# Moving a second level of Strassen from layer 1's fifth product to layer 2's first and fifth products

## The chip, the cores and the metric

The kernel runs on one core of a Trainium2 chip. The metric is the device time of one execution in microseconds (us). The numbers of the profile come from one profiled execution of the same program.

## The reference

Sparse attention over 4 x 8 heads of 768 tokens gives x, 3072 tokens by D = 512. Eight experts (F = 1024) then work on all tokens, and their outputs are added with weights P that come out of eight rounds of row and column scaling:

```python
    logits = x @ w_gate
    P = np.exp(logits - logits.max())
    for _ in range(8):
        P /= P.sum(1, keepdims=True) + 1e-09
        P /= P.sum(0, keepdims=True) + 1e-09
        P *= N / E
    for e in range(E):
        h = np.maximum(x @ w1[e], 0.0)        # layer 1: [3072,512] x [512,1024]
        ye = h @ w2[e]                        # layer 2: [3072,1024] x [1024,512]
        out += P[:, e:e + 1] * ye
```

## The kernel before

**Stages.** Attention and expert 0 take the first part of the span, and the scaling of P follows beside the first products of expert 1. From there on experts 1 to 7 run, in products of fp16 matmuls summed in fp32. This second part is what the change touches.

**Strassen, first level.** Both layers of experts 1 to 7 use the Winograd form of Strassen's algorithm: the operands are cut into 2 x 2 quarters (A11 to A22 the stationary ones, B11 to B22 the moving ones), sums S1 to S4 and T1 to T4 of quarters are formed by VectorE, and seven products p1 to p7 (layer 1) or q1 to q7 (layer 2) take the place of eight. In layer 1 a unit is an expert e, a block j of 512 tokens in each half of the tokens (NJ = 3 blocks), and half u of the hidden columns; a unit, called a *duo*, has two sides k, and each product of a side is two matmuls of 512 columns (`product1`, line 991). There are 42 duos, six for each expert. In layer 2 a pair (e, j, c) is the token tile c of block j and its partner in the other half; each of its seven products is four matmuls of 256 columns (`product2`, line 997). There are four pairs in a block, so two for each duo.

**Strassen, second level.** In `duo`, `second` computes the first product (names ending in m) or the fifth (ending in n) of both sides together by seven pieces instead of eight: each piece is one matmul of 256 columns (line 1050). It starts with piece 1 in one bank, ScalarE copies the half (`fd`, line 1059) into a second bank and `fh` (line 1070) sets another half aside; VectorE adds halves in the joins j1 and j2 (`plus`, line 938). m is used from block (1, 2) on, in 38 duos, and n from block (2, 1) on, in 34. Its sums of weights (`wa_sum`) and of tokens (`xa_sum`) for n (g = 1) live in unused rows of out_acc.

**Banks.** PSUM has eight banks here: ab (three, layer 1's products), g (two, layer 1's second accumulators), x (two) and y (one) for layer 2. After products, ScalarE copies (c5, c2, c1, seeds, v6, r11, r21) and VectorE adds with a clip at zero (`relu_plus`, line 941, c12 and c22) or adds halves (v5). Results hf of layer 1 lie in the tile hs (seven quarters A11, A12, S3, A22, S1, S2, S4), of which there are four.

**Outputs.** For experts 2 to 7 ScalarE scales each quarter by P (`part`, line 1265) into rows c and HT + c of out_acc, and GpSimd's queue adds them to the output in DRAM by DMA (`da` line 1286, `db` line 1289). So most of out_acc is free scratch in these experts. The last block fetches its rows back (`fetch`, line 1242), adds there with VectorE, and stores.

**The order of the work.** `Plan.order` is a planner that runs when the program is built: each step is `put` with an engine, an estimated cost from the table `us`, the steps it depends on, the banks it opens and uses, and a priority. It emits the steps in the order in which its model starts them; every engine then takes its own in that order. Priorities come from the table `PR` (one number for each kind of step). `feed(n)` puts duo n, the weight loads and sums for the next expert and the pairs of duo n - 2, three duos ahead of the one being emitted.

Of the kernel before, what the change touches and what calls it, by code (L numbers as in the profile page):

```python
# [10 lines left out]
FP32 = mybir.dt.float32  # L11
# [129 lines left out]
def kernel(  # L141
# [10 lines left out]
    nc = tc.nc  # L152
# [767 lines left out]
    if True:  # L920
# [107 lines left out]

        def wa_sum(g, e, u, n):
            if n == 0:  # L1030
                wa[g, e, u] = (spare16(HT + 4 + (2 * e + u) % 3, 384).rearrange("p (s f) -> p s f", s=3) if g else
                               late.tile([128, 3, 128], FP16, tag="wa", name="wa", bufs=3))
# [137 lines left out]
        def pair(e, j, c, spare=False, tail=False, c1_at=None):  # L1170
            def h(q):
                return lambda f: hs[e, j, f // 2][:, q, f % 2, :]
            ta, tb = 4 * j + c, HT + 4 * j + c
            B = {}
# [54 lines left out]
            def add_to(t, k, src):  # L1229
                acc = out_acc[:, t, k * DH:(k + 1) * DH]  # L1230
                nc.vector.scalar_tensor_tensor(out=acc, in0=at(src), scalar=P_sb[:, t, e:e + 1], in1=acc,
                                               op0=ALU.mult, op1=ALU.add)
# [4 lines left out]
            def store(t, k=slice(0, DM), eng=nc.sync):  # L1237
                eng.dma_start(out=rows(t)[:, k], in_=out_acc[:, t, k])

            def fetch():  # L1240
                for t in (ta, tb):
                    nc.sync.dma_start(out=out_acc[:, t, :], in_=rows(t))

            def add_less(src):
                acc = out_acc[:, tb, 0:DH]
                nc.vector.scalar_tensor_tensor(out=acc, in0=at(src), scalar=nP_sb[:, tb, e:e + 1], in1=acc,
                                               op0=ALU.mult, op1=ALU.add)
# [46 lines left out]
            def fin():  # L1294
                nc.gpsimd.tensor_tensor(out=out_acc[:, tb, 0:DH], in0=out_acc[:, tb, 0:DH], in1=out_acc[:, tb, DH:DM],
                                        op=ALU.add)
                store(tb)

            def ahead():
                nc.gpsimd.tensor_tensor(out=out_acc[:, tb, 0:DH], in0=out_acc[:, tb, 0:DH], in1=out_acc[:, tb, DH:DM],  # L1300
                                        op=ALU.add)

            def z3():
                nc.scalar.activation(out=out_acc[:, HT + 7, c // 2 * DH:(c // 2 + 1) * DH], in_=at(3), func=AF.Copy, scale=P_sb[:, ta, e:e + 1])
# [5 lines left out]
            def z0():  # L1310
                nc.vector.scalar_tensor_tensor(
                    out=out_acc[:, tb, 0:DH], in0=at(2), scalar=P_sb[:, tb, e:e + 1],
                    in1=out_acc[:, tb, 0:DH], op0=ALU.mult, op1=ALU.add)

            def z4():
                nc.gpsimd.tensor_tensor(out=out_acc[:, ta, DH:DM], in0=out_acc[:, ta, DH:DM], in1=out_acc[:, HT + 7, c // 2 * DH:(c // 2 + 1) * DH], op=ALU.add)
# [5 lines left out]
            def x1():  # L1322
# [3 lines left out]
            return {f.__name__: f for f in (scale_a, scale_b, q1, c1, q5, v5, q6, v6, q2, q7, q3, q4, y0, y1, y2, y3, fin, ahead, fetch, e0, e1, e2, e3, e4,  # L1326
                                            da, db, dc,
                                            z3, z2, z0, z4, x0, x1)}

        us = dict(m=0.1092, p=0.4316, q=0.4368, seed=0.55, c5=0.5, c2=0.49, r=0.49, c12=0.607, c22=0.607, s=0.6,  # L1330
                  c1=0.34, v6=0.28, v5=0.35, y=0.395, half=0.275, join=0.335, w1=0.205, w2=0.6, wa=0.14, x=0.6,
# [138 lines left out]
        for u in course:  # L1470
# [7 lines left out]
        plan.more({"x": 2, "y": 1, "c1": 1, "m5": 1, "n5": 1})  # L1478
        plan.ring["ab"].append(None)

        PR = {
# [13 lines left out]
        pairs = {}  # L1495

# [3 lines left out]
        def w_sums(e, i, prio, old=()):  # L1500
            for n in range(4):
                WT[e, i, n] = put("DVE", us["w1"], lambda n=n: w1_sum(e, i, n),
                                  [WT.get((e, i, n - 1)), U["w1", e, i], *old], prio + 0.01 * n)

# [20 lines left out]
        def pair_users(e, j, names=("q1", "q2", "q3", "q4", "q5", "q6", "q7")):  # L1525
            return [pairs[e, j, c][q] for c in range(4) for q in names] if (e, j, 0) in pairs else []

        def plan_pair(e, j, c, prio):
# [5 lines left out]
            f, d = pair(e, j, c, spare, last_block, c1_at), {}  # L1534
# [5 lines left out]
            def op(name, eng, cost, deps, opens=(), uses=(), p=None):  # L1540
# [7 lines left out]
            op("q1", "PE", m, of("r110", "r111") + [U["w2", e]] + ([src[1]["c121"], src[1]["r211"]] if spare else []),  # L1548
               [bx])
            op("c1", "ACT", us["c1"], ["q1"] + ([src[1]["c121"], src[1]["c221"]] if spare else []), c1s, [bx])  # L1550
            op("q5", "PE", m, ["q1", W2[e, 0]] + of("s1"), (), [bx])
            op("v5", "DVE", us["v5"], ["q5", "c1"], [by], [bx] + c1s)
# [11 lines left out]
            if spare:  # L1564
                op("ahead", "POOL", 0.75, [pairs["in", c]], p=0)
                op("z3", "ACT", us["part"], ["q3"], (), [by], p=1)
# [5 lines left out]
            elif e == 1 or last_block:  # L1572
# [7 lines left out]
                else:  # L1580
                    pairs["ys", c] = pairs["st", c] = landed([d["y2"], d["y3"]], 4.0)
            else:
                free = [pairs["ys", c]] if e > 2 or j else [pairs[1, 0, c]["landed"]]
                op("e0", "ACT", us["part"], ["q2"] + free, (), [bx], p=PR["yd"])
                op("e2", "ACT", us["part"], ["q7"] + free, (), [by], p=PR["yd"] + 2)
                if e < E - 1:
                    op("e1", "ACT", us["part"], ["q4"] + free, (), [bx], p=PR["yd"] + .1)
                else:
                    op("e4", "DVE", us["y"], ["q4", "e2"] + free, (), [bx], p=PR["yd"] + 2)
                op("e3", "ACT", us["part"], ["q3"] + free, (), [by], p=PR["yd"] + 2.1)  # L1590
                op("da", "POOL", us["da"], ["e0", "e3"], p=PR["yd"] + 3)
                op("db", "POOL", us["da"], ["e1" if e < E - 1 else "e4", "e2"]
                   + ([pairs["dc", j, c]] if e == E - 1 else []), p=PR["yd"] + 3)
                pairs["ys", c] = landed([d["da"], d["db"]], 4.0)
                if e == E - 2 and j < NJ - 1:
                    op("dc", "POOL", us["da"], [pairs["ys", c]], p=PR["yd"] + 160)
                    pairs["dc", j, c] = landed([d["dc"]], 4.0)
                if e == E - 2 and j == NJ - 1:
                    op("fetch", "SP", 0.2, [pairs["ys", c]], p=PR["yd"])
                    pairs["in", c] = landed([d["fetch"]], 4.0)  # L1600
# [4 lines left out]
            if e == 1:  # L1605
                d["landed"] = pairs["ys", c]
# [5 lines left out]
        def feed(n):  # L1612
            base = 10000.0 + 100.0 * n
            if n < len(duos):
# [7 lines left out]
                for g, h, since in ((0, "m", (1, 2)), (1, "n", (2, 1))):  # L1622
# [4 lines left out]
                def prio(name):  # L1627
                    if name in ("s1", "s3", "s2", "s4"):
                        return base + PR["S"] + 0.1 * ("s1", "s3", "s2", "s4").index(name)
                    return base + PR[{"p10": "m1", "p11": "m4"}.get(name, name)]  # L1630
# [10 lines left out]
                if n == 7:  # L1641
                    p5s = ("p50", "p51")
                    held = [pairs[1, 1, c]["landed"] for c in range(4)]
                    for v in range(2):
                        wa_sums(1, 2, v, base + 30 + 10 * v, held + users(2, 0, v, p5s))
                    for m, i in enumerate((1, 2, 0)):
                        xa_sums(1, i, base + 50 + 70 * m, held + users(*((2, 0) if i == 0 else (1, i)), 0, p5s)
                                + users(*((2, 0) if i == 0 else (1, i)), 1, p5s))
                if e + 1 < E:
# [11 lines left out]
                    if k == 5:  # L1661
                        w_sums(e + 1, 1, w - 100, users(e, 2, 0))
                        for g in (0, 1) if e > 1 else (0,):
                            wa_sums(g, e + 1, 0, w - 90, users(e - 1, 2, 1))
# [3 lines left out]
                        for g in (0, 1) if e > 1 else (0,):  # L1668
                            wa_sums(g, e + 1, 1, w + 20, users(e, 2, 0))
            m = n - 2  # L1670
            if m < len(duos):
# [45 lines left out]
```

## Time and profile before

| | |
|---|---|
| median of 3 runs (lowest to highest) | 664.56 us (664.53 to 665.34) |
| the profiled execution | 664.45 us, its span 662.7 us |
| TensorE, weight loads, VectorE, ScalarE, GpSimd busy | 652.9, 456.8, 506.0, 533.2, 260.0 us |
| matmuls of layer 2 (line 997) | 2352 of 128x256, 273 ns each |
| matmuls of layer 1 (line 991) | 888 of 128x512, 379 or 380 ns each |
| pieces of the second level (line 1050) | 504 of 128x256, 273 ns each |
| joins m (pab<-pab,m) and n (pab<-pab,out_acc) | 76 and 68, 427 and 431 ns each |
| half copies (line 1059; line 1070 to m and to out_acc) | 72; 38 and 34, 380 ns each |
| layer 1's sums (hf<-hf 128x1024) | 126 and 42, 687 and 682 ns each |
| granted TensorE clock | 0.999 |

Busy times are sums in which overlapping instructions of one engine count once. Successive matmuls overlap: each one's row holds its passage through the array, so the distance between starts, not the length, is what one costs in a stream. In the chain that ended last, TensorE has 89% of the span.

### The profile page before, as it was taken

To read this page: it belongs to the slowest core of one execution; us is meant where nothing else is said; L and a number is where in the kernel's file an instruction comes from. 1 tells how busy PE (TensorE), PEld (TensorE's weight loads), DVE (VectorE), ACT (ScalarE), POOL (GpSimd) and SP (SyncE) were. 2 spreads that over 40 slices of the span, in tenths; PEclk is the share of its full clock that TensorE was granted. 3 is DMA by queue.
4 is the path that set the end of the run, shared out by engine and by line. 5 is a ranking of instruction groups with operands and counts; after the bars stand their busy time and mean duration, and the time that the engine had idled before them with its cause. 6 is when DMAs were issued, how large, how long until landed. Compare 5 with 4: busy or idle time off the path is not lost.

```text
span 662.7 us, 14448 instructions
## 1 busy us (share of the span) xinstructions
PE 652.9 (99%) x5293; PEld 456.8 (69%) x5293; DVE 506.0 (76%) x1304; ACT 533.2 (80%) x1189; POOL 260.0 (39%) x322
## 2 busy tenths in 40 slices
PE   8999999999999999999999999999999999999996
PEld 4766656555677677777777777777777777777775
DVE  7889998579889987685767767866768576776674
ACT  6776766556995678998989989899899898998872
POOL 8699504223011022444343342534343445533322
PEclk9999999999999999999999999999999999999999
DMA  9999958600627268986979697988898598988676
GB/s 162 185 153 148 143 82 82 87 2 1 111 98 142 96 121 122 126 106 83 170 100 132 87 156 97 128 101 117 135 126 111 74 185 114 153 137 175 90 90 165
DMA packets 147078, 77.70 MB, mean 117 GB/s; under 512 B 112704, under 2 KB 124736, under 8 KB 147008
## 3 DMA queue, kind: packets, MB, share of 16 engines
q0 software_dynamic: 124864, 62.64, 81.2%
q1 hardware_dynamic: 21184, 13.42, 8.1%
q8 instruction: 41, 0.67, 0.4%
q10 hardware_dynamic: 960, 0.74, 0.4%
q14 instruction: 29, 0.24, 0.1%
HBM read 55.59 MB, written 45.09 MB: 152 GB/s over the span
## 4 chain that ended last, share of the span: by engine, by line
PE 89%; DVE 8%; DMA 1%; issue 0%; ACT 0%; DVEq 0%
PE px L997 21%; PE pg L991 16%; PE py L997 16%; PE pab L991 12%; PE pab L1050 8%; PE yps L236 5%; PE hps L226 5%; DVE xs L552 1%; DMA kT<-kst 1%; PE sg L388 1%; PE idle L597 1%; PE tkq L354 1%; DVE em L440 1%; DVE km L382 1%; PE pab L997 1%
## 5 line engine op out<-in xcount | busy, mean ns | idle before, releaser
L997 PEld LDWEIGHTS <-hf 128*128 128x128 f16 x2352 | 229.9, 98 | 79.5 <-issue 0.8
L1289 POOL DMA_DIRECT2D out_dram<-out_acc x68 | 60.0, 883 | 209.3 <-ACT out_acc L1265 193.1
L997 PE MATMUL px<-w,hf 128*128 128x256 f16 x656 | 98.3, 273 | 0.0
L997 PE MATMUL px<-ws,hf 128*128 128x256 f16 x656 | 97.8, 273 | 0.0
L997 PE MATMUL py<-w,hf 128*128 128x256 f16 x656 | 91.2, 273 | 0.0
L935 DVE TENSOR_TENSOR hf<-hf 128x1024 f16<-128x1024 f16 x126 | 83.4, 687 | 0.5
L1265 ACT ACTIVATE out_acc<-py,P_sb 128x256 f32<-128x256 f32 x136 | 61.2, 476 | 24.2 <-PE py L997 21.6
L941 DVE CUSTOM_DVE_ANT_0 hf<-pab,c 128x512 f16<-128x512 f32 x84 | 57.8, 689 | 25.8 <-ACT c L1123 12.4
L1286 POOL DMA_DIRECT2D out_dram<-out_acc x68 | 69.0, 1014 | 20.4 <-ACT out_acc L1265 19.4
L991 PEld LDWEIGHTS <-w 128*128 128x128 f16 x520 | 50.9, 98 | 20.4
L941 DVE CUSTOM_DVE_ANT_0 hf<-pg,c 128x512 f16<-128x512 f32 x84 | 57.7, 686 | 9.4 <-ACT c L1116 5.9
L938 DVE TENSOR_TENSOR pab<-pab,out_acc 128x256 f32<-128x256 f32 x68 | 29.3, 431 | 43.9 <-PE pab L1050 43.9
L938 DVE TENSOR_TENSOR py<-px,c 128x256 f32<-128x256 f32 x82 | 35.0, 427 | 35.9 <-PE px L997 34.9
L202 POOL DMA_DIRECT2D w<-in_moe_w_dram x56 | 44.2, 862 | 42.4 <-PE pg L991 40.9
L991 PE MATMUL pab<-xT,w 128*128 128x512 f16 x184 | 54.6, 380 | 0.0
L217 ACT ACTIVATE hf<-pg 128x512 f16<-128x512 f32 x84 | 50.6, 607 | 4.5 <-PE pg L991 1.8
L1123 ACT COPY c<-pg 128x512 f32<-128x512 f32 x84 | 50.1, 596 | 4.5 <-PE pg L991 2.6
L1108 ACT COPY pg<-pab 128x512 f32<-128x512 f32 x84 | 50.4, 601 | 2.7 <-PE pab L1050 2.7
L217 ACT ACTIVATE hf<-pab 128x512 f16<-128x512 f32 x84 | 50.4, 601 | 2.4 <-PE pab L991 1.8
L1116 ACT COPY c<-pab 128x512 f32<-128x512 f32 x84 | 49.0, 583 | 3.3 <-PE pab L991 2.4
L991 PE MATMUL pab<-xT,ws 128*128 128x512 f16 x168 | 50.0, 379 | 0.0
L991 PE MATMUL pg<-xT,w 128*128 128x512 f16 x168 | 50.0, 379 | 0.0
(191 smaller groups left out, 1388.8 us busy)
## 6 DMA issues: line engine op xcount, KB each, us to landing
out_dram<-out_acc POOLq DMA_DIRECT2D x136, 256.0 KB, 5.3
w<-in_moe_w_dram POOLq DMA_DIRECT2D x8, 1024.0 KB, 9.5
w<-in_moe_w_dram POOLq DMA_DIRECT2D x56, 128.0 KB, 5.7
out_dram<-out_acc SPq DMA_DIRECT2D x28, 256.0 KB, 2.3
vx<-in_v_dram POOLq DMA_DIRECT2D x16, 192.0 KB, 5.7
qst<-in_q_dram POOLq DMA_DIRECT2D x31, 96.0 KB, 5.3
kst<-in_k_dram POOLq DMA_DIRECT2D x24, 96.0 KB, 5.2
out_acc<-out_dram SPq DMA_DIRECT2D x8, 256.0 KB, 4.3
```

What stands on the lines that cost most here:

```text
L217: nc.scalar.activation(out=out, in_=in_, func=AF.Relu, bias=0.0, scale=1.0)
L935: nc.vector.tensor_tensor(out=out, in0=in0, in1=in1, op=ALU.subtract)
L938: nc.vector.tensor_tensor(out=out, in0=in0, in1=in1, op=ALU.add)
L941: nc.vector._custom_dve(TENSOR_ADD_SAT, out=out, in0=in0, in1=in1, s0=FLT_MAX, s1=0.0)
L991: nc.tensor.matmul(bank[:], lhsT=w[:, dk, :], rhs=x[:, dk, :], start=start and dk == 0, stop=dk == KH - 1, skip_group_check=True)
L997: nc.tensor.matmul(bank, lhsT=a(f)[:, 128 * c:128 * (c + 1)], rhs=w[:, f, :], start=start and f == 0, stop=f == FH - 1, skip_group_check=True)
L1050: nc.tensor.matmul(B[bank][:, lo:lo + 256], lhsT=weight1a(g, w, e, u), rhs=moving1a(g, v, j), start=start, stop=True, skip_group_check=True)
L1108: nc.scalar.copy(out=B["g" + K][:], in_=B["a" + K][:])
L1123: nc.scalar.copy(out=B["c2" + K][:], in_=B["g" + K][:])
L1265: nc.scalar.activation(out=out_acc[:, (c, HT + c)[t == tb], k * DH:(k + 1) * DH], in_=at(src), func=AF.Copy, scale=scale[:, t, e:e + 1])
L1286: nc.gpsimd.dma_start(out=rows(ta), in_=out_acc[:, c, :], accum_op=ALU.add)
L1289: nc.gpsimd.dma_start(out=rows(tb), in_=out_acc[:, HT + c, :], accum_op=ALU.add)
```

## The change

Layer 2's first and fifth products of two token tiles c and c + 2 are computed together by a second level (`twin`): the quarters are the two tiles (rows), the two halves of the hidden columns, and the two halves of 128 output columns. One bank holds q1 in its first half and q5 in its second, and each of the seven pieces n1 to n7 is four matmuls of 128 columns (two products, two parts of the sum). Two copies (nd, nh) and two joins (j1, j2) lie between them, as in layer 1. After them the pairs go on as before with c1, v5, q6 and so on. Twins are used in blocks (2, 1) to (7, 1); blocks of expert 1, (2, 0) and the last block keep four matmuls for each product.

VectorE forms the sums: `h_sub`, four for each block, over 128x1024 elements, and `w2_sub`, eight for each expert, over 128x256. S1, S2, S4 lie in three rows of out_acc; S3 takes the place of quarter A21, whose block's later products do not read it. The sums of w2 lie in other rows of out_acc.

Layer 1's fifth product goes back to two matmuls of 512 columns a side; its sums of weights and tokens for g = 1 are gone. PSUM has ab with two banks instead of three, y with two instead of one. The last block's tiles live in other rows of out_acc (`home`), and its `fetch` is put with tiles 0 and 2 of block (7, 1) instead of with the pairs of block (6, 2). `z3` waits for the matmuls of block (7, 1). The table PR has a number for each kind of step and an added one for each of the six duos of an expert (`rank`).

The core of the diff:

```diff
+        LAST_A, LAST_B = (11, 21, 0, 2), (20, 22, 12, 23)
+        def h_sub(e, j, n):
+            own = hs[e, j, 0][:, A11:S1 + 1:S1 - A11, :, :], hs[e, j, 1][:, A11:S1 + 1:S1 - A11, :, :]
+            m = {"A11": own[0][:, :, :, 0:256], "A21": own[0][:, :, :, 256:512], "S3": own[0][:, :, :, 256:512],
+                 "A12": own[1][:, :, :, 0:256], "A22": own[1][:, :, :, 256:512]}
...
+            f(m[o], m[a], m[b])
+        def twin(e, j, c, b0, b1):
...
+            def piece(b, k, w, v, start=False):
+                for g in range(2):
+                    for i in range(2):
+                        nc.tensor.matmul(half(b, k)[:, g, :], lhsT=still2(e, j, g, w, c)[:, i, :],
+                                         rhs=moving2a(e, g, v)[:, i, :], start=start and g == 0 and i == 0,
+                                         stop=i == 1, skip_group_check=True)
-        plan.more({"x": 2, "y": 1, "c1": 1, "m5": 1, "n5": 1})
-        plan.ring["ab"].append(None)
+        plan.more({"x": 2, "y": 2, "c1": 1, "m5": 1, "n5": 1, "k9": 1})
+        TWIN = (2, 1), (E - 1, NJ - 2)
+        def rank(name, k):
+            return PR[name] + PR.get(f"{name}.{k}", 0.0)
+        def plan_twin(e, j, c, prio):
...
+            op("n1", "PE", us["n"], [src[0][x] for x in ("r110", "r111", "s1")] + [W2[e, 0], pairs.get("nd")], [b0])
+            op("nd", "ACT", us["half"], ["n1"], [b1], [b0])
+            op("n5", "PE", us["n"], ["n1", s[0], *t[0]], (), [b0])
+            op("nh", "ACT", us["half"], ["n5"], [kh], [b0])
+            op("n2", "PE", us["n"], ["nd"] + [src[1][x] for x in ("r110", "r111", "s1")], (), [b0])
+            op("n6", "PE", us["n"], ["nd", s[1], *t[1]], (), [b1])
+            op("j1", "DVE", us["join"], ["n6", "nh"], (), [b0, b1, kh])
+            op("n3", "PE", us["n"], ["j1", s[3]], (), [b0])
+            op("n7", "PE", us["n"], ["j1", s[2], *t[2]], (), [b1])
+            op("j2", "DVE", us["join"], ["n7"], (), [b1, kh])
+            op("n4", "PE", us["n"], ["j2", *t[3]], (), [b1])
+            for k in range(2):
+                plan_pair(e, j, c + 2 * k, prio + rank(f"q{k}", 2 * j + c),
+                          (built[k], (b0, b1)[k], ([d["n2"], d["n3"]], [d["n4"]])[k]))
...
-                for g, h, since in ((0, "m", (1, 2)), (1, "n", (2, 1))):
+                for g, h, since in ((0, "m", (1, 2)),):
...
+                if u and TWIN[0] <= (e, j) <= TWIN[1]:
+                    h_sub_sums(e, j, base + rank("NS", j))
+                if e >= 2 and (n == 8 or e > 2 and (j, u) == (0, 0)):
+                    w2_sub_sums(e, base + PR["NW"], [pairs[1, NJ - 1, 3]["landed"]] if n == 8 else [])
-            if m < len(duos):
+            if m < len(duos) and TWIN[0] <= duos[m][:2] <= TWIN[1]:
+                plan_twin(*duos[m], base)
+            elif m < len(duos):
```

More of the change, by code (lines that the diff above doesn't have):

```diff
@@ L1173, in pair @@
             ta, tb = 4 * j + c, HT + 4 * j + c
+            home = {ta: LAST_A[c], tb: LAST_B[c]} if tail else {ta: ta, tb: tb}
             B = {}
@@ new lines, in still2, with w2_subs @@
+        def still2(e, j, g, what, c):
+            lo = 128 * (c % 2)
+            if what in ("S1", "S2", "S4"):
+                return h_subs(e, j)[:, ("S1", "S2", "S4").index(what), g, :, lo:lo + 128]
+            lo += 256 if what in ("A21", "S3", "A22") else 0
+            return hs[e, j, int(what in ("A12", "A22"))][:, (A11, S1)[g], :, lo:lo + 128]
+        def w2_subs(e, g):
+            if e % 2 == 0:
+                a = spare16((11, HT + 11)[g], 1024)
+            elif g:
+                a = spare16(HT + 7, 1024)
+            else:
+                a = out_acc[:, HT + 4:HT + 7, :].rearrange("p t f -> p (t f)").bitcast(FP16)[:, 1152:2176]
+            return a.rearrange("p (s k f) -> p s k f", s=4, k=2)
@@ new lines, in moving2a, with w2_sub @@
+        def moving2a(e, g, what):
+            if what[0] == "T":
+                return w2_subs(e, g)[:, int(what[1]) - 1]
+            k = 2 if what in ("B21", "B22") else 0
+            o = 128 if what in ("B12", "B22") else 0
+            return ws2[e][:, 0, k:k + 2, o:o + 128] if g else w2s[e][:, k:k + 2, o:o + 128]
+        def w2_sub(e, g, n):
+            m = {w: moving2a(e, g, w) for w in "B11 B12 B21 B22 T1 T2 T3 T4".split()}
+            sub(*[m[w] for w in (("T1", "B12", "B11"), ("T2", "B22", "T1"), ("T3", "B22", "B12"),
+                                 ("T4", "B21", "T2"))[n]])
@@ new lines, in twin, with half, open_bank, n1 @@
+        def twin(e, j, c, b0, b1):
+            B = {}
+            def half(b, k):
+                return b["x"][:].rearrange("p (g k f) -> p g k f", g=2, k=2)[:, :, k, :]
+            def open_bank(b):
+                b["x"] = xps.tile([128, 512], FP32, tag=f"x{plan.now.pop(0)}", name="px", bufs=1)
+            def piece(b, k, w, v, start=False):
[4 more added lines that the diff above has]
+                                         stop=i == 1, skip_group_check=True)
+            def n1():
+                open_bank(b0)
+                piece(b0, 0, "A11", "B11", True)
+            def nd():
+                open_bank(b1)
+                nc.scalar.copy(out=half(b1, 0), in_=half(b0, 0))
+            def n5():
+                piece(b0, 1, "S1", "T1")
+            def nh():
+                plan.now.pop(0)
+                B["held"] = out_acc[:, 7, 256:512].rearrange("p (g f) -> p g f", g=2)
+                nc.scalar.copy(out=B["held"], in_=half(b0, 1))
+            def n2():
+                piece(b0, 0, "A12", "B21")
+            def n6():
+                piece(b1, 0, "S2", "T2")
+            def j1():
+                plus(half(b0, 1), half(b1, 0), B["held"])
+            def n3():
+                piece(b0, 1, "S4", "B22")
+            def n7():
+                piece(b1, 0, "S3", "T3")
+            def j2():
+                plus(half(b1, 1), half(b1, 0), B["held"])
+            def n4():
+                piece(b1, 0, "A22", "T4")
+            return {f.__name__: f for f in (n1, nd, n5, nh, n2, n6, j1, n3, n7, j2, n4)}
@@ L1503, in w_sums, with h_sub_sums, w2_sub_sums @@
                                   [WT.get((e, i, n - 1)), U["w1", e, i], *old], prio + 0.01 * n)
+        HS2, W2A = {}, {}
+        def h_sub_sums(e, j, prio):
+            src = [made[e, j, 0], made[e, j, 1]]
+            first = [pairs[1, NJ - 1, c]["landed"] for c in range(3)] if e == 2 else []
+            HS2[e, j] = s = []
+            for n, more in enumerate((first + [src[1][x] for x in ("s1", "r110", "r111")] + [src[0][x] for x in ("s1", "r110", "r111")], [],
+                                      [src[0]["s2"], src[0]["s3"]], [])):
+                s.append(put("DVE", us["ns"], lambda n=n: h_sub(e, j, n), s[-1:] + more, prio + 0.01 * n))
+        def w2_sub_sums(e, prio, old=()):
+            for g in range(2):
+                for n in range(4):
+                    W2A[e, g, n] = put("DVE", us["nw"], lambda g=g, n=n: w2_sub(e, g, n),
+                                       [W2A.get((e, g, n - 1)), W2[e, 0], *old], prio + 0.01 * n + 0.1 * g)
         def wa_sums(g, e, u, prio, old=()):
@@ L1533, in plan_pair @@
                 c1_at = lambda: fast.tile([128, 512], FP32, tag=("c2", "c5")[c // 2], name="c1t", bufs=1)[:, 0:DH]
-            f, d = pair(e, j, c, spare, last_block, c1_at), {}
+            f, d = second[0] if second else pair(e, j, c, spare, last_block, c1_at), {}
             src = [made[e, j, 0], made[e, j, 1]]
@@ L1591, in plan_pair @@
-                op("da", "POOL", us["da"], ["e0", "e3"], p=PR["yd"] + 3)
+                    op("e4", "DVE", us["y"], ["q4", "e2"] + free, (), [bx], p=rank("yd", 4 * j + c) + 2)
+                op("e3", "ACT", us["part"], ["q3"] + free, (), [by], p=rank("yd", 4 * j + c) + 2.1)
+                op("da", "POOL", us["da"], ["e0", "e3"], p=rank("yd", 4 * j + c) + 3)
                 op("db", "POOL", us["da"], ["e1" if e < E - 1 else "e4", "e2"]
-                   + ([pairs["dc", j, c]] if e == E - 1 else []), p=PR["yd"] + 3)
```

134 lines of the change are left out of this document (81 added, 53 removed), and 76 rows, old and new, of the table PR.

## The prediction

> **What bounds the kernel now.** I read the engine shares first, then busy time over the stretch in which the change acts, then TensorE's waits, and last the order of matmuls inside that stretch.
>
> ```profile
> PE 652.9 (99%) x5293; PEld 456.8 (69%) x5293; DVE 506.0 (76%) x1304; ACT 533.2 (80%) x1189; POOL 260.0 (39%) x322
> ```
>
> ```profile
> 250.00:640.00 390.00, 390.00 (x2933) 286.41 (x2931) 279.15 (x642) 349.90 (x841) 153.88 (x182) 1.00 0.88 122
> ```
>
> ```profile
> PE pab L1050 <- DVE pab L938: 0.2, 1, 0.2
> ```
>
> The first line is the page's, the second the busy times from 250 to 640 us (PE, PEld, DVE, ACT, POOL), the third the only wait of TensorE after its first 120 us. In that stretch TensorE has no gap, at full clock; ScalarE is busy 89.7% (349.90/390), VectorE 71.6%. A busy row of matmuls overlaps itself (each lasts 273 ns but they start 109 ns apart), so I test it by starts:
>
> ```profile
> 404.81 0.60 PE L997 MATMUL px<-ws,hf 128*128 128x256 f16 x4
> 405.25 1.04 PE L997 MATMUL py<-w,hf 128*128 128x256 f16 x8
> 406.12 0.59 PE L991 MATMUL pab<-xT,w 128*128 128x512 f16 x2
> ```
>
> Columns are start and length; 406.12 - 404.81 is 1.31 us for twelve 256-column matmuls: 0.109 each. Pairs of 512 columns (L991) take 0.433 us there, 0.2165 each. A duo (two token-tile pairs of layer 2 and one unit of layer 1) has 56 + 14 matmuls of 256 columns and 20 of 512: 70 x 0.109 + 20 x 0.2165 = 11.96 us. The chain of waits shows the same py products at 309.70, 321.66 and 333.64: a period of 11.96 us. So the stretch has no slack: what TensorE has to issue is the time, and what it saves ends the kernel earlier, as long as nothing makes it wait.
>
> **The price of a 128-column matmul.** The whole change rests on it, since layer 2's pieces go from 256 to 128 columns, each with its own weight load. Layer 2 before shows none, but attention does:
>
> ```profile
> 60.94 0.50 PE L354 MATMUL tkq<-ident,qst 128*128 128x128 bf16 x6
> 61.28 0.51 PE L398 MATMUL vs<-vx,m_blk 128*128 128x128 bf16 x6
> 61.62 1.03 PE L236 MATMUL yps<-w,h 128*128 128x512 f16 x4
> ...
> 65.17 0.51 PE L354 MATMUL tkq<-ident,kst 128*128 128x128 bf16 x6
> 65.51 0.50 PE L354 MATMUL tkq<-ident,qst 128*128 128x128 bf16 x6
> 65.85 0.74 PE L573 MATMUL lp<-wg_bf,xT 128*128 128x8 f16 x24
> 66.45 0.32 PE L226 MATMUL hps<-xT,w 128*128 128x384 f16 x1
> ```
>
> Six go by in 0.34 us (60.94, 61.28, 61.62; again 65.17, 65.51, 65.85): 0.0567 each, with one load per matmul. A line through 0.109 at 256 and 0.2165 at 512 gives 0.0553 at 128. I take 0.056 and keep 0.0553 and 0.0567 as ends. Loads alone go faster: 24 matmuls of 8 columns, each with its load, pass in 66.45 - 65.85 = 0.60 us, 25 ns each.
>
> The Trainium skill (TensorE: Matmul & The Clock Gate, Back-to-back issue gap) says that a real stream of weight loads and matmuls holds about 81 ns each at 128 columns, more than the 56 ns of isolated ones; by that figure the change would be an estimated 20 us slower (28 x 0.081 against 1.744, 32 times, and 3.5). The rows above, loads included, disagree with it.
>
> **The change, part by part.**
>
> *Layer 2, q1 and q5 in a twin.* Two token tiles had 2 x 2 x 4 = 16 matmuls of 256 columns: 16 x 0.109 = 1.744 us. A twin has 7 products x 2 x 2 = 28 of 128 columns: 28 x 0.056 = 1.568. It saves 0.176, and there are 32 twins (blocks (2,1) to (7,1) are 16, two twins each): -5.6 us (-6.3 at 0.0553, -5.0 at 0.0567).
>
> *Layer 1's fifth whole.* The n product of a unit had 7 x 0.109 = 0.763 us; whole it is 4 x 0.2165 = 0.866. That costs 0.103 in each of the 34 duos that had it (the 68 joins pab<-pab,out_acc are two each): +3.5 us.
>
> TensorE's sum: -2.1 us (-2.8 to -1.5). Break-even is a piece price of (1.744 - 3.5/32)/28 = 0.0584 us, so the direct rows leave only 3% of room.
>
> *ScalarE.* Out go 34 x 2 half copies (380 ns, L1059 and L1070), in come 32 x 2 (nd, nh) of the same size; c1 stays one per tile. Nothing changes beyond 68 against 64 copies. It stays at 90%, hidden beside TensorE as now.
>
> *VectorE.* Joins: 68 out, 64 in, 0.43 us each. Out per expert: 8 sums wa of g=1, at 0.219: 1.75 us. In per expert of three blocks: 12 sums h_sub of 128x1024 (row hf<-hf, 687 ns): 8.24 us, and 8 sums w2_sub of 128x256 (row ws<-w, 285 ns): 2.28. Net 8.8 us more per six duos (71.8 us): 71.6% becomes 84%. Beside TensorE this costs nothing if it spreads; its cover is VectorE's idle time, 28% now. Uncovered it costs what a sum lasts, 0.69 us at a time. VectorE takes its instructions in order: behind four sums (2.75 us) stand c12, c22, v5 and the joins j1, j2, for which TensorE waits. The window 322 to 334 us has 10.02 us of VectorE work in 12 already; a block's sums fit only in its neighbours with 7.5. I take zero to 0.34 us per block, and zero as likeliest.
>
> *PSUM.* ab goes from 3 banks to 2, y from 1 to 2. A unit's first product needs both ab banks while its split runs, then seed, p2, r11; I bound the hold by the rows: some 3 us for the split's round trips (four matmul stages of about 0.3, copies 0.38, joins 0.43 twice), then 0.6 + 0.6 + 0.6, then b: 0.6 + 0.6 + 0.7 with matmuls between, in all about 8 us of a 11.9 us period. The x pair: split, c1 (0.40), v5 (0.43), two products, two scalings (0.48): about 6 of 11.9. Neither is full, and with the second bank y never holds. Value 0; bounds -0.4 us (one join's wait less at the start) to +2 us (one ScalarE queue late in each of a few duos).
>
> *Order.* Every step after 180 us moves. PE's order before leaves 0.2 us of waits there, so an order cannot gain; it can only lose.
>
> *The end.* The last block's tiles move to other rows of out_acc, and its fetches (eight, 4.3 us to landing, on SP from 587.45 us before) wait: the last two for the landing of tiles 0 and 2 of block (7,1). Before, POOL's adds of that block go out at 636, 641 and 647 us; with 5.3 to landing, four issues of 0.34 and 4.3, data is there at about 647, and the last block's tiles 2 and 3 first use it at 648 to 650. SP has nothing else queued until 650.40. Margin 1 to 3 us; cost 0, at worst +2.
>
> Sum: the profiled execution took 664.45 us (span 662.7 and 1.75 around it), 0.11 below the median of 664.56. 664.45 - 2.1 = 662.35, near 662.4 on the median's scale. About 0.2% (1.3 us) is what a measurement of this kernel can tell from no change.
>
> **The rivals.**
>
> 1. *Gaps of the new order eat the gain* (same). With ScalarE at 90% and VectorE at 84%, an order written ahead by estimates drifts. For: peaks of 10 us in 12. Against: 0.2 us of gaps now. One gap of 0.06 us in each of 32 duos gives 1.9 us back: 664.3.
>
> 2. *VectorE's sums hold TensorE* (slower). Place: the four h_sub sums of each of 16 blocks, ahead of joins and evictions. Price: half a sum, 0.34 us, per block, 5.5 us in all: 664.45 - 2.1 + 5.5 = 667.9. It eats the gain from 0.13 us a block on and is slower by 0.2% from 0.21. For: 84% and the strict queue. Against: TensorE has two duos of work in hand.
>
> 3. *The loads set the pace* (slower). A load row lasts 98 ns; if it showed whole, 28 x 0.098 - 1.744 = 1.0 us per twin, 32 + 3.5 = 35 us: 700; half shown, near 682. Against: the rows of 25 and 57 ns with a load each. For: those runs are six long, and attention's. The Trainium skill's 81 ns (the page and section above) would be this rival.
>
> 4. *The end waits for its fetches* (same): 2 us, 664.4.
>
> **How the numbers follow.** Forecast 0.52 (661.3 to 663.2, likeliest 662.4); rival 1 0.16; rival 2 0.22; rival 3 0.06; rival 4 0.04. Faster 0.52, same 0.20, slower 0.28. The range reaches from 661.3 (0.0553 a piece, and 0.4 at the start) to 668.0 (rival 2 at its price); outside are rival 3 and the worse part of rival 2.
>
> **What would show it.** The 128x128 rows of layer 2 should number 896 and start 0.056 us apart; a duo should take 40 x 0.109 + 28 x 0.056 + 7 x 0.109 + 24 x 0.2165 = 11.89 us; VectorE should stand at 84% with ScalarE at 90%; TensorE's waits should stay under 1 us after 250 us. Wrong: a start distance over 0.058, waits of PE px on DVE h_sub or join rows, or a last block whose first adds wait for a DMA.

## The result, and the profile after

The changed kernel takes 667.43 us (median, 665.13 to 671.63), beside 664.77 us for the kernel before on the same chip: a ratio of 1.0048, 95% interval 1.0026 to 1.0071. Run again beside other kernels, it had 1.0024 (1.0010 to 1.0039). So it is slower by 0.2 to 0.5% where I forecast 0.3% faster. The profiled execution took 669.53 us, its span 667.6, its clock 0.995.

The page's shares and the busy times from 250 to 640 us (PE, PEld, DVE, ACT, POOL) answer to the two lines shown of before:

```profile
PE 652.6 (98%) x5575; PEld 447.4 (67%) x5575; DVE 543.6 (81%) x1352; ACT 531.4 (80%) x1185; POOL 260.4 (39%) x322
```

```profile
250.00:640.00 390.00, 389.51 (x3219) 277.09 (x3217) 320.63 (x708) 349.93 (x842) 154.67 (x182) 1.00 0.87 119
```

In the stretch that the change is about nothing went wrong: TensorE is busy 389.51 of 390 us, ScalarE exactly as before (349.93), VectorE at 320.63/390 = 82%, where I forecast 84%. The loss is not there. TensorE's waits say where it is (total, times, longest, in us):

```profile
PE px L997 <- DVE out_acc L1275: 3.8, 1, 3.8
PE vs L398 <- DMA vx<-in_v_dram: 1.4, 1, 1.4
...
PE px L1397 <- DVE px L938: 0.4, 1, 0.4
```

One wait of 3.8 us, once. (The 1.4 us lie in attention, ahead of all that the change touches: they come and go between executions of the same program.) The trace in order of time (start, length, engine) shows the end of the scaling of P, the pieces, and the wait (lines between are left out at "..."):

```profile
162.28 0.28 PE L1537 MATMUL sink<-csum_sb,col_en 128*128 128x8 f32 x2
...
394.83 0.28 PE L1397 MATMUL px<-w,hf 128*128 128x128 f16 x2
394.94 0.27 PE L1397 MATMUL px<-ws,hf 128*128 128x128 f16 x2
395.05 0.39 PE L1397 MATMUL px<-out_acc 128*128 128x128 f16 x4
395.28 0.27 PE L1054 MATMUL pab<-xa,w 128*128 128x256 f16 x1
...
643.70 1.77 SPq L1247 DMA_DIRECT2D out_acc<-out_dram  x4
...
651.45 0.60 PE L997 MATMUL py<-w,hf 128*128 128x256 f16 x4
...
651.96 0.72 POOL L1306 TENSOR_TENSOR out_acc<-out_acc 128x256 f32<-128x256 f32 x1 [7.06 <-DMA out_acc<-out_dram]
652.71 0.48 DVE L1236 SCALAR_TENSOR_TENSOR out_acc<-pg,P_sb,out_acc 128x256 f32<-128x256 f32 x1 [6.24 <-POOL out_acc L1306]
...
655.33 0.47 DVE L1275 SCALAR_TENSOR_TENSOR out_acc<-px,nP,out_acc 128x256 f32<-128x256 f32 x1
655.86 0.60 PE L997 MATMUL px<-w,hf 128*128 128x256 f16 x4 [3.81 <-DVE out_acc L1275]
...
660.22 1.04 PE L997 MATMUL py<-w,hf 128*128 128x256 f16 x8
```

Eight pieces pass in 395.28 - 394.83 = 0.45 us, 0.056 each, with a load for every one: the price that the change rests on is as forecast. Then read upwards from 655.86. TensorE stands for VectorE's L1275; VectorE, which takes its queue in order, has six additions to the last block ahead of L1275 (it empties the bank px), and stood 6.24 us itself for GpSimd's L1306; that stood 7.06 us for the fetch that SP (the sync engine) issued from 643.70 on. One DMA holds three engines in turn.

To compare kernels I use two marks that every one has: the last `sink` matmul (160.00 before, 162.28 after), up to which the program is the same, and the start of TensorE's last group (655.41 before, 660.22 after). In the trace of before they are

```profile
160.00 0.28 PE L1427 MATMUL sink<-csum_sb,col_en 128*128 128x8 f32 x2
...
655.41 1.04 PE L997 MATMUL pg<-w,hf 128*128 128x256 f16 x8
```

Between them lie 495.41 us before and 497.94 after, 2.53 more. This *stretch* leaves out the 2.28 us of the profiled execution that chance put ahead of the first mark. Each stretch is that of one profiled execution.

| kernel | median us | ratio to before, 95% interval | stretch us | last group to end of span us |
|---|---|---|---|---|
| before | 664.77 to 665.25 | | 495.41 | 7.3 |
| after | 667.43 | 1.0048 (1.0026 to 1.0071) | 497.94 | 7.4 |
| again (after, unchanged) | 666.89 | 1.0024 (1.0010 to 1.0039) | 498.12 | 7.4 |
| early_fetch | 664.73 | 0.9994 (0.9985 to 1.0003) | 494.27 | 8.3 |
| short_sums | 665.78 | 1.0007 (0.9994 to 1.0020) | 496.84 | 7.3 |
| fifth_whole (from before) | 677.50 | 1.0181 (1.0165 to 1.0198) | | |
| late_fetch (from before) | 671.49 | 1.0094 (1.0076 to 1.0111) | 499.59 | 10.2 |
| early_short | 663.85 | 0.9981 (0.9973 to 0.9990) | 493.88 | 8.4 |
| spare_last | 664.70 | 0.9992 (0.9983 to 1.0000) | 494.16 | 8.3 |
| double_sums | 703.57 | 1.0573 (1.0558 to 1.0588) | | |
| early_load | 663.75 | 0.9978 (0.9968 to 0.9987) | 493.35 | 7.7 |
| pool_s4 | 688.70 | 1.0349 (1.0333 to 1.0366) | | |
| pool_s4_load | 687.54 | 1.0330 (1.0313 to 1.0348) | | |

Each ratio is to runs of the kernel before on the same chip: again, early_fetch, short_sums and fifth_whole shared one, so did late_fetch, early_short, spare_last and double_sums, and the last three.

### The profile page after: what moved, and what is told of

Same layout as the page of the kernel before. It is cut to its first block, busy times and chain, and to the rows that moved or that the text cites. A ratio compares the mean times of both kernels' runs of the same rounds, so it can differ in the third digit from the quotient of the medians.

```text
span 667.6 us, 15025 instructions
## 1 busy us (share of the span) xinstructions
PE 652.6 (98%) x5575; PEld 447.4 (67%) x5575; DVE 543.6 (81%) x1352; ACT 531.4 (80%) x1185; POOL 260.4 (39%) x322
## 4 chain that ended last, share of the span: by engine, by line
PE 84%; DVE 6%; DMA 3%; issue 3%; POOL 1%; ACT 1%; POOLq 0%; DVEq 0%
PE pab L991 16%; PE pg L991 16%; PE py L997 15%; PE px L997 12%; PE px L1397 7%; PE yps L236 5%; PE hps L226 5%; PE pab L1054 4%; DVE xs L552 1%; DMA kT<-kst 1%; DMA vx<-in_v_dram 1%; DMA w<-in_moe_w_dram 1%; PE sg L388 1%; PE tkq L354 1%; DVE em L440 1%
## 5 line engine op out<-in xcount | busy, mean ns | idle before, releaser
L997 PEld LDWEIGHTS <-hf 128*128 128x128 f16 x1840 | 178.7, 98 | 52.8 <-issue 4.3
L935 DVE TENSOR_TENSOR hf<-hf 128x1024 f16<-128x1024 f16 x142 | 94.2, 688 | 2.2
L997 PE MATMUL py<-w,hf 128*128 128x256 f16 x656 | 92.5, 273 | 0.0
L991 PEld LDWEIGHTS <-ws 128*128 128x128 f16 x504 | 47.3, 98 | 33.5 <-issue 0.3
L1270 ACT ACTIVATE out_acc<-py,P_sb 128x256 f32<-128x256 f32 x136 | 63.5, 486 | 7.0 <-PE py L997 5.2
L202 POOL DMA_DIRECT2D w<-in_moe_w_dram x56 | 46.8, 935 | 51.8 <-PE pg L991 49.8
L991 PEld LDWEIGHTS <-w 128*128 128x128 f16 x520 | 49.2, 98 | 21.2 <-issue 1.1
L997 PE MATMUL px<-w,hf 128*128 128x256 f16 x400 | 59.5, 273 | 3.8 <-DVE out_acc L1275 3.8
L997 PE MATMUL px<-ws,hf 128*128 128x256 f16 x400 | 59.7, 273 | 0.0
L991 PE MATMUL pab<-xT,w 128*128 128x512 f16 x184 | 53.9, 379 | 0.0
L1112 ACT COPY pg<-pab 128x512 f32<-128x512 f32 x84 | 50.2, 597 | 4.7 <-PE pab L1054 4.3
L1397 PEld LDWEIGHTS <-hf 128*128 128x128 f16 x512 | 38.7, 98 | 17.4
L991 PE MATMUL pg<-xT,w 128*128 128x512 f16 x168 | 50.0, 379 | 0.0
L991 PE MATMUL pab<-xT,ws 128*128 128x512 f16 x168 | 50.0, 379 | 0.0
```

The lines of the kernel that those rows point to most:

```text
L935: nc.vector.tensor_tensor(out=out, in0=in0, in1=in1, op=ALU.subtract)
L991: nc.tensor.matmul(bank[:], lhsT=w[:, dk, :], rhs=x[:, dk, :], start=start and dk == 0, stop=dk == KH - 1, skip_group_check=True)
L997: nc.tensor.matmul(bank, lhsT=a(f)[:, 128 * c:128 * (c + 1)], rhs=w[:, f, :], start=start and f == 0, stop=f == FH - 1, skip_group_check=True)
L1112: nc.scalar.copy(out=B["g" + K][:], in_=B["a" + K][:])
L1270: nc.scalar.activation(out=out_acc[:, (c, HT + c)[t == tb], k * DH:(k + 1) * DH], in_=at(src), func=AF.Copy, scale=scale[:, t, e:e + 1])
L1397: nc.tensor.matmul(half(b, k)[:, g, :], lhsT=still2(e, j, g, w, c)[:, i, :], rhs=moving2a(e, g, v)[:, i, :], start=start and g == 0 and i ...
```

## The experiments

**First four: is it the end, or VectorE's sums?** My theory after the traces was that TensorE's work fell as worked out and that the late fetch eats it; the rival was my own rival 2, the sums on VectorE. The unchanged kernel ran again beside them.

> The changed kernel once more, nothing edited, for a second trace. If the end is the cause (the last block's fetch comes too late and stands in VectorE's queue), TensorE waits 3 to 5 us on an out_acc add after 645 us here too, and the time is 666 to 670 us. If the 1.4 us wait for the first vx load at 7 us in the first trace was chance, it is missing from about half the traces and the clock of such a run is about 0.998; if it belongs to the program, it is here again. If VectorE's sums are the cause, waits of px on VectorE rows fill the stretch from 250 to 640 us.

It took 666.89 us. The same wait stood in its trace, shorter, and something came behind it (windows of 2 us: busy PE, PEld, DVE, ACT, POOL, then the granted clock, as a share of full speed):

```profile
PE px L997 <- DVE out_acc L1275: 2.3, 1, 2.3
```

```profile
650.00:652.00 2.00, 0.00 (x0) 0.00 (x0) 1.97 (x5) 1.17 (x3) 1.54 (x3) 1.00 0.64 99
652.00:654.00 2.00, 1.78 (x14) 1.52 (x14) 1.19 (x4) 0.64 (x3) 2.00 (x3) 0.85 1.05 271
654.00:656.00 2.00, 2.00 (x12) 1.39 (x10) 0.93 (x4) 0.23 (x1) 0.27 (x1) 0.50 1.11 139
656.00:658.00 2.00, 2.00 (x16) 1.64 (x15) 1.31 (x4) 0.36 (x1) 0.00 (x0) 0.79 1.09 274
658.00:660.00 2.00, 1.29 (x12) 0.91 (x10) 1.56 (x5) 0.00 (x0) 0.83 (x2) 1.00 0.93 315
```

After the pause the clock falls to one half for about 3 us, and the groups there start 0.86 us apart in place of 0.44: 1.7 us more by the distances of starts. So the end costs 2.3 + 1.7 = 4 us here, and 3.8 in the first execution, where the clock stayed up.

The fetches made early, other rows for the last block:

```diff
-        LAST_A, LAST_B = (11, 21, 0, 2), (20, 22, 12, 23)
+        LAST_A, LAST_B = (11, 21, 4, 6), (20, 22, 5, 23)
...
-                        old = ((pair_users(E - 1, 0) + pair_users(E - 2, NJ - 1)) if c == 0 else
-                               [pairs[E - 1, NJ - 2, x]["landed"] for x in (0, 2)])
+                        old = pair_users(E - 1, 0) + pair_users(E - 2, NJ - 1)
```

> The last block's tiles 2 and 3 live in rows 4, 5 and 6 of out_acc, which nothing uses by then, and their fetches no longer wait for the landing of block (7, 1); TensorE's order is unchanged. End theory: the 3.8 us wait at 652 us is gone and the kernel is 3.5 to 4.5 us faster than the changed one, 663.0 to 663.8 us, which is 0.1 to 0.3% under the kernel before. Rival (VectorE's sums hold TensorE): less than 1 us faster than the changed kernel, 666.5 us or more.

664.73 us: the wait is gone and the stretch is 498.12 - 494.27 = 3.85 us shorter than in the unchanged kernel. The median gained 2.2 us, less than the expected 3.5 to 4.5. The profiled spans also differ by 2.2: 3.85, less 1.0 because the last group now stands that much further from the end of the span, less 0.7 that chance put ahead of the first mark.

The sums cut to a sixteenth (`f(*[m[x][:, :, :, 0:16] for x in (o, a, b)])`, and `still2` reading quarters that are there):

> The four sums h_sub of each block work on 16 of 256 columns in each run and the pieces read other quarters in place of S1, S2 and S4, so the outputs of the blocks with twins are not the reference's; the order on every engine is as in the changed kernel. VectorE loses 64 x about 0.55 us = 35 us of work. End theory: the stretch from 250 to 640 us gets at most 1 us shorter, the wait at the end stays, 666 to 667.5 us. Rival (VectorE's sums hold TensorE, half a sum or more per block): 4 us or more faster, 663 us or less.

665.78 us, 1.1 less than the unchanged kernel: just under the 666 to 667.5 of the end theory, and far from the 663 of the rival. The wait at the end stays (2.8 us).

One half of the change alone on the kernel before, layer 1's fifth product whole, without its sums:

```diff
-                for g, h, since in ((0, "m", (1, 2)), (1, "n", (2, 1))):
+                for g, h, since in ((0, "m", (1, 2)), (1, "n", (E, 0))):
```

> The kernel before with layer 1's fifth product whole in every duo and the sums for it left out, planned anew with its own priorities. By the sum of the prediction, 34 x (4 x 0.2165 - 7 x 0.109) = 3.5 us slower than the kernel before: 668.2 us, ratio 1.0053. If the second level in layer 1 saved less than its columns say (its joins and copies holding TensorE), the ratio is nearer 1.000.

677.50 us, 12.3 more than before, far past the expected 3.5. Added up by the distances of starts, TensorE's issue grew by 3.4 us, as worked out; the rest, some 9 us, is TensorE standing between groups (its list of waits names 3.6 us of it), in an order that the planner made anew with the old priorities. The expectation held the work and forgot the order. That the priorities are to blame is likely but not shown: no run sets them anew for this edit.

**Then four: the price of the end on the old kernel, and of the sums by doubling them.** The kernel before, with nothing of the change but the homes of the last block and the moment of its fetches (the second four now go to rows that block (7, 1) still stores from):

```diff
+            home = {ta: (8, 9, 0, 2)[c], tb: (20, 21, 12, 23)[c]} if tail else {ta: ta, tb: tb}
...
-                    op("fetch", "SP", 0.2, [pairs["ys", c]], p=PR["yd"])
-                    pairs["in", c] = landed([d["fetch"]], 4.0)
+                    pairs["of", c] = pairs["ys", c]
+                if e == E - 1 and j == NJ - 2 and c in (0, 2):
+                    for n in ((0, 1), (2, 3))[c // 2]:
+                        get = pair(E - 1, NJ - 1, n, tail=True)["fetch"]
+                        pairs["in", n] = landed([put("SP", 0.2, get, [pairs["of", n]] + [pairs["ys", x] for x in (0, 2) if c],
+                                                     prio + PR["yd"])], 4.0)
```

> The kernel before with only the homes of the last block's tiles and its fetches changed as in the kernel after: the second four fetches go to rows that block (7,1)'s pairs 0 and 2 still store from, so that they wait for those stores. TensorE's order is that of before down to the last 100 instructions. That the late fetches are the cost at the end: TensorE waits 2 to 4 us near 650, and the kernel takes 667 to 669 with no other part of the change in it. That the end is late only because of the twins (VectorE's queue): no wait over 0.5 us there, at most 665.5.

671.49 us, 6.5 more than before, past the expected 2 to 4. The chain in time:

```profile
648.37 1.19 POOL L1290 DMA_DIRECT2D out_dram<-out_acc  x1
652.64 1.97 SPq L1243 DMA_DIRECT2D out_acc<-out_dram  x4
657.85 0.48 DVE L1232 SCALAR_TENSOR_TENSOR out_acc<-pab,P_sb,out_acc 128x256 f32<-128x256 f32 x1 [1.55 <-DMA out_acc<-out_dram]
657.96 0.72 POOL L1317 TENSOR_TENSOR out_acc<-out_acc 128x256 f32<-128x256 f32 x1 [6.04 <-DMA out_acc<-out_dram]
659.11 0.36 ACT L1216 COPY pg<-pg 128x256 f32<-128x256 f32 x1 [3.65 <-POOL out_acc L1317]
659.52 1.03 PE L997 MATMUL pg<-w,hf 128*128 128x256 f16 x8 [2.13 <-ACT pg L1216]
```

The store is issued at 648.37, the fetch follows at 652.64, the data is used at 657.85, and ScalarE and TensorE wait behind it. The stretch grew by 4.2 us and the part after it by 2.9. So the late fetch alone makes the old kernel slower by more than the whole change does. It is a harder case than the changed kernel's, though: the fetch goes out at 652.64, behind two stores in SP's queue, where the changed kernel has it at 643.70. It shows the mechanism without the twins, not the price that the changed kernel pays.

Fetches early and sums short together:

> Early fetches and short sums together: the last block's rows as in early_fetch, and each sum h_sub done on 16 of its 256 columns, with the pieces reading quarters that are already there (the output is therefore not the reference's; TensorE's and ScalarE's work, their order and every transfer are those of early_fetch). That the new order costs TensorE small gaps through VectorE, beside the wait at the end: the two savings add, 664.7 (early_fetch) less the 1.1 us that short sums took off the unchanged kernel, near 663.6, with under 1 us of gaps left between 250 and 640 us. That the short sums only eased VectorE at the very end (the same microseconds that early_fetch took away): 664.7, and the gaps at 290 and 504 us stay.

663.85 us, as expected from adding the two: 0.9 under early_fetch (0.7 when each is taken against before on its own chip), and 0.2% faster than before. The trace says less: the stretch is 0.4 us shorter, and two waits for joins are still in it,

```profile
289.14 0.27 PE L1397 MATMUL px<-w,hf 128*128 128x128 f16 x2 [0.40 <-DVE px L938]
...
360.92 0.27 PE L1397 MATMUL px<-w,hf 128*128 128x128 f16 x2 [0.32 <-DVE px L938]
```

each behind a weight sum of VectorE that stood 2.6 or 2.7 us for its load. TensorE's order is that of early_fetch, so the starts can be compared one by one, each counted from the first mark: 0.7 us is gained at 504 us, 1.0 lost at these two waits, and 0.7 gained in small steps elsewhere. The small steps (0.6 us in short_sums) are what the sums themselves cost, about 0.04 us a block; the rest depends on when a load lands in that execution.

The last block's pairs in the old order (`"l1": 662.3` to 3662.3, `"l3": 342.2` to 3342.2):

> Early fetch, and the last block's four pairs done in the order of the kernel before: plain ones (c 0 and 2) first, the two that end with 128 KB stores (c 1 and 3) last, by two priorities of the order (l1 and l3 up by 3000). That the order of the pairs sets the last 7.55 us: the time after the last matmul falls to the 6.5 us of the kernel before, near 663.7. That the moved pairs make TensorE wait for joins in their own banks: no gain, 664.7 or more. Nothing before 640 us changes.

664.70 us, no gain: the part after the last group stayed at 8.3 us, though VectorE and the last store were done 1 us earlier than in the kernel before (a store from ScalarE's queue issued at 657.31 beside 658.34). The order of the pairs is not what sets that part; what does stays open.

Every sum twice, early fetch otherwise:

```diff
             f(m[o], m[a], m[b])
+            f, o, a, b = ((plus, "S1", "A21", "A22"), (sub, "S2", "S1", "A11"), (sub, "S2", "S1", "A11"),
+                          (sub, "S4", "A12", "S2"))[n]
+            f(m[o], m[a], m[b])
```

> Early fetch with every sum h_sub done twice (S1, S2 and S4 over again, S2 also in place of S3, which is not idempotent): 64 more of 0.69 us on VectorE, 44 us, its share between 250 and 640 us from 82% to about 93%. Nothing else differs. That VectorE has room and only a few sums lie uncovered: 1 to 2 us more than early_fetch, 665.7 to 666.7. That the sums stand ahead of joins in VectorE's queue and hold TensorE (half a sum, 0.34 us, more for each of 16 blocks): 5.5 us more, 670.

703.57 us, 38.8 more than early_fetch. Both sides of the expectation missed by a wide margin. The 64 added sums are 44 us of VectorE, so 88% of them lie bare on the path:

```profile
PE pab L1054 <- DVE pab L938: 11.0, 15, 1.3
PE px L1400 <- DVE out_acc L935: 9.9, 11, 1.1
PE px L1400 <- DVE px L938: 7.1, 6, 1.5
```

```profile
391.21:469.73 78.52, 72.76 (x595) 50.84 (x595) 66.97 (x145) 65.27 (x157) 27.97 (x33) 1.00 0.81 109
```

TensorE waits for the doubled sums themselves (out_acc L935) and for joins behind them (L938). Six duos, which take 71.4 us in early_fetch, now take 78.52, 7.1 more for three blocks with 4 x 0.687 = 2.75 us more each: of 2.75 us a block absorbs 2.75 - 7.1/3 = 0.4. And yet VectorE is busy only 66.97 of those 78.52 us, 85%. In this order, which was planned for single sums, the room beside the unchanged sums is 0.4 us in a block, although VectorE's idle time there is 18%.

**Last three: what is left in the stretch.** In early_fetch the largest remaining wait of TensorE, and what stands before it on VectorE:

```profile
503.33 0.29 DVE L938 TENSOR_TENSOR ws<-w 128x256 f16<-128x256 f16 x1 [1.12 <-DMA w<-in_moe_w_dram]
...
503.87 0.42 DVE L938 TENSOR_TENSOR px<-px,out_acc 128x256 f32<-128x256 f32 x1
...
504.35 0.27 PE L1397 MATMUL px<-w,out_acc 128*128 128x128 f16 x2 [0.67 <-DVE px L938]
```

A sum of the next expert's weights waits for its load, and the twin's join stands behind it. So the fourth weight tile is loaded along with the third, into a free row; no engine's order changes but GpSimd's by this one load (other weight loads go out up to 3 us earlier as well, since their buffers come free sooner):

```diff
+        if e > 2 and i == 3:
+            if (e, i) in w1s:
+                return
+            t = out_acc[:, HT + 4 if e == E - 1 else 4 + e % 2, :].bitcast(FP16)
+            t = w1s[e, i] = t.rearrange("p (k h f) -> p k h f", k=KD, h=2)
...
+        if e > 2 and i == 2:
+            load_w1(e, 3)
```

> Early fetch, and the fourth weight tile of layer 1 of experts 3 to 7 loaded together with the third, some 10 us earlier, into a row of out_acc that is free (rows 4, 5 and 16); nothing else in any engine's order changes. That the gaps of 0.5 to 0.8 us per run near 504 us (and its like at other experts) come from a sum that waits for this load: they go, 664.0 to 664.3, 0.5 us under early_fetch. That they come from the sums h_sub ahead in VectorE's queue: the gaps stay, 664.7.

663.75 us, a little more gain than expected, and this kernel beats both: 0.9978 of the time before, interval 0.9968 to 0.9987, with nothing left out. The load's wait is gone (the join's piece starts at 502.40 without one), and TensorE's list of waits names nothing after attention any more. Counted from the first mark, TensorE's matmuls start as in early_fetch up to that piece and 0.9 us earlier from it on: the gain is this one wait.

```profile
159.77 0.28 PE L1545 MATMUL sink<-csum_sb,col_en 128*128 128x8 f32 x2
...
501.79 0.43 DVE L946 TENSOR_TENSOR px<-px,out_acc 128x256 f32<-128x256 f32 x1
...
502.13 0.28 DVE L943 TENSOR_TENSOR out_acc<-out_acc 128x256 f16<-128x256 f16 x1
...
502.40 0.28 PE L1405 MATMUL px<-w,out_acc 128*128 128x128 f16 x2
...
653.12 1.04 PE L1005 MATMUL py<-w,hf 128*128 128x256 f16 x8
```

Its stretch is 493.35 us, 2.06 under the kernel before: the -2.1 of the prediction's sum. By the medians the kernel is 1.3 us under before; the part after the last group takes 0.4 of the difference, and the rest lies between single executions and medians.

One of the four sums moved to GpSimd, at the same place of the order, alone and with the early load:

```diff
+            if n == 3:
+                return nc.gpsimd.tensor_tensor(out=m[o], in0=m[a], in1=m[b], op=ALU.subtract)
```

> Early fetch, with the last of a block's four sums (S4 = A12 - S2, 128x1024) done by POOL at the same place of the order, 16 in all: VectorE has 11 us less. That VectorE's place in front of joins is what costs: near 663.9, most of the 0.9 us that the short sums took off. That POOL is late with it (its sums of 128x256 take 0.72 us, so this one 1.5 to 3 us, ahead of its store issues): TensorE waits for S4 in each block, 0.3 us or more each, 669 or above.

> The edits of early_load and pool_s4 in one kernel, each as described for itself. If both gaps are what they are taken for: 663.4 to 663.7, faster than the kernel before by about 0.2%. If POOL's sums are late: as pool_s4, 669 or above, whatever the load does.

688.70 and 687.54 us, as the second side expected and far worse. GpSimd's sum has a mean of 2.69 us against VectorE's 0.68, and it holds VectorE too:

```profile
261.94 3.70 POOL L1356 TENSOR_TENSOR out_acc<-hf,out_acc 128x1024 f16<-128x1024 f16 x1 [0.68 <-DVE out_acc L935]
...
264.08 1.72 DVE L935 TENSOR_TENSOR out_acc<-w 128x256 f16<-128x256 f16 x1
...
265.70 0.23 PEld L1399 LDWEIGHTS <-out_acc 128*128 128x128 f16 x4 [1.27 <-POOL out_acc L1356]
265.70 0.28 PE L1399 MATMUL px<-w,out_acc 128*128 128x128 f16 x2 [0.78 <-POOL out_acc L1356]
265.72 0.28 DVE L935 TENSOR_TENSOR out_acc<-ws 128x256 f16<-128x256 f16 x1
```

A VectorE sum that takes 0.28 us elsewhere takes 1.72 and ends within 0.2 us of GpSimd's. The Trainium skill (GPSIMD Engine Reference, Specifications) says that GpSimd shares its SBUF interfaces with VectorE and contends with instructions that read two operands from SBUF; these two rows agree.

## Why the prediction was wrong, point by point

**Right: the price of a piece and TensorE's sum.** 896 pieces of 128 columns at 0.056 us; six duos in early_load take 473.95 - 402.55 = 71.40 us between the same py groups, 11.90 a duo (forecast 11.89). In all, 512 fewer matmuls of L997, 238 fewer of the pieces of layer 1, 136 more of L991 and 896 new ones are -55.8 - 25.9 + 29.4 + 50.2 = -2.1 us. Rival 3 falls with that. Beside the 81 ns that I set against these rows, the same page of the Trainium skill (TensorE: Matmul & The Clock Gate, Wait — 56ns, not 53.3ns?) gives 55.6 ns for 128 columns at full clock; the trace agrees with that section, loads included.

**Right: ScalarE, VectorE's share, PSUM.** 349.93 against 349.90 us; 82% against 84%; no wait on y or ab of more than 0.2 us.

**Wrong: "The end. Margin 1 to 3 us; cost 0, at worst +2".** This is the term that turned the sign. It measured 3.8 us in one execution and 2.3 + 1.7 in the other; taking it away shortens the stretch by 3.85, and a later fetch still, put into the old kernel, costs 6.5. Rival 4 was the right mechanism at half its price, and had 4 in 100. In before's time (2.28 us less than in the trace of after, by the first marks) the fetch went out as worked out: 643.70 - 2.28 = 641.4, where 636 + 5.3 gives 641.3. Three steps behind that failed. I took 4.3 us from issue to landing, the median of before; the fetches after took up to 6.8, four at once beside GpSimd's adds, so the data was there at 651.96 - 2.28 = 649.7 and not at 647. I had the first use at 648 to 650; in early_fetch, where no data is late,

```profile
646.76 0.48 DVE L1236 SCALAR_TENSOR_TENSOR out_acc<-pg,P_sb,out_acc 128x256 f32<-128x256 f32 x1 [1.74 <-PE pg L997]
```

it comes at 646.76 - 0.82 = 645.9 by the same marks. So the data was 3.8 us late where I had it 1 to 3 early. And I priced the wait alone: behind it on VectorE stood six additions ahead of the one that empties TensorE's bank, so the 652.0 of the data (the trace's own time) became 655.9 for TensorE, and the clock could fall behind that.

**Half right: VectorE's sums (rival 2).** "Zero to 0.34 us per block, zero as likeliest" held in the end: with the load mended, all sums kept, the stretch gives the whole -2.1. By the traces of the short sums the bare part of them is 0.6 to 0.7 us in all, 0.04 us a block (short sums and the early load in one kernel were not run). But the reason I gave, "its cover is VectorE's idle time, 28%", is refuted by double_sums: the cover was 0.4 us a block, and 2.4 of the next 2.75 us lie bare. With one more sum of 0.69 us in a block rival 2 at its 0.34 us would have been near; that is an estimate from these two numbers.

**Rival 1, gaps of the order**, took 0.9 us (494.27 of early_fetch against 493.35 of early_load), near half the gain, and could be mended. (TensorE's order is another from 163.6 us of before on, not from 180; nothing rests on it.) The stretch then has -2.1 for the work, +0.9 for the load's gap and +3.7 to +3.9 for the end, which makes +2.5 and +2.7. These are differences of the same stretches, so their sum proves nothing. What stands by itself is that the first, measured as 493.35 - 495.41 = -2.06, meets the -2.1 counted from matmuls, and that TensorE's list of waits names 3.8 us for the end. The medians of the two runs say +2.7 and +1.6.

## What to carry to other kernels

When an edit saves little on the busiest engine, price the transfers that it delays before the work that it saves: a fetch that waits for a store pays both landings, by the slow ones and not the median, and then all that is queued behind its first user. Free time on an in-order engine is no cover by its share; double the work in doubt and see what part of it shows. And when a saving does not arrive, take what stands beside it one piece at a time: here some rows of a buffer, which the change had moved, and a load whose user on VectorE stands ahead of a join held the gain back.

## What the hardware showed that I had not expected

After a pause of TensorE of 2.3 us the granted clock fell to 0.50 for some 3 us, and after one of 2.8 us in short_sums it fell too, while after one of 3.8 us, in another execution of the first program, it stayed at 1.00. The Trainium skill (TensorE: Matmul & The Clock Gate, What's actually happening) puts the fall behind an idle window of about 3.4 us; these three executions do not bear out a length at which it must come.

One GpSimd sum of 128x1024 took 2.69 us in the mean, up to 3.7, and stretched VectorE's 0.28 us to 1.72 beside it.
